# An attention and mixing kernel on one core: fixing the order in which TensorE issues, in long runs

## The chip, the cores and the metric

The kernel runs on one core of a Trainium2 chip. The metric is the device time of one execution in microseconds (us), of which the median of several runs is given. A profile of one execution shows what each engine did: TensorE (PE in the profile, and PEld for its weight loads), VectorE (DVE), ScalarE (ACT), GpSimd (POOL) and SyncE (SP), which issues the transfers.

## The reference

Eight batches of eight heads with 576 positions of 64 numbers go through causal attention with a window of 128 positions and a bias that falls with distance. The heads, side by side, are an x of 576 by 512 for each batch, and this x is mixed:

```
rel    = pos[:, None] - pos[None, :]
mask   = (rel >= 0) & (rel < 128)
scores = where(mask, q @ k.T / 8 - slope[h] * abs(rel), -1e9)
x      = softmax(scores) @ v                      # heads side by side: 576 x 512
theta  = x @ w_theta
y      = w_tok_r @ (x * cos(theta)) + w_tok_i @ (x * sin(theta))
u      = x + y
out    = u + max(u @ w_ch, 0)
```

## The kernel before, in words

The work of a batch has four stages, and the stages of neighbouring batches overlap.

**Attention**, in pairs of heads, four pairs to a batch (`attend`). For one pair: the scores (`Pair.scores`, L345 for the 64 last positions and L359 for the rest, 15 pieces of work in three calls that `SCORES` names), each with three products of rounded parts; the bias and the row minimum on DVE (`weigh`, L374, which reads the PSUM tile `s_ps`); the exponential on ACT (L377); the transposes of the weights (`flip`, L382, 16 for a pair in four banks), which ACT copies to half precision (L389) and DVE to the rest of it (L390); and for each of the two heads 27 products with v (`values`, L418) into the one PSUM tile `acc`, which DVE reads to divide by the sum (`finish`, L424 to L427) before the next head may write it. The scores of a pair are computed one pair ahead.

**The turn** (`turn`), once the four pairs of a batch are done: for each of five pieces i = 1, 2, 3, 4, 0 of the positions, four transposes of x (`columns`, L449), twelve products with w_theta (`products`, L469; eight for piece 0), and cosine and sine (`angle`, L480 to L501): ACT and DVE fold the angle into a turn (L483, L484, L486), ACT takes two sines (L490, L491), DVE multiplies them with x (L494), and each result is split into z_hi on ACT (L440) and z_lo on POOL (L441). Piece 0 is split apart from the others: L480, L481, L483, L484, L486, L490, L491, L498, L499, then z_hi on ACT (L500) and z_lo on DVE (L501). Pieces 1 to 4 give the chunks 0 to 7 of z, piece 0 gives chunk 8.

**Mixing** (`mix`): eight groups of 27 products (L530), three for each of the nine chunks in the order 0, 4, 1, 5, 2, 6, 3, 7, 8. Chunk 8 is the last of each group. When a group is done DVE adds it to x (L535), and ACT and POOL split the sum (L537, L538).

**Channels** (`channels`): eight groups of twelve products (L551), each closed by DVE (L554) and written out (L556).

While the pairs of batch b+1 are in `attend`, the mixing of batch b runs beside them, and the channels of batch b beside the turn of batch b+1. The table of ACT's functions is loaded twice for a batch: for the sines and, behind the last sine (`behind`), for the exponentials.

A scheduler orders each engine's instructions from the order of the program, priorities and its own estimate of times. Before, the priorities MIX, CHAN and ROTATE shift mixing, channels and turn against the attention, and `step(other, 6)` hands out pieces of mixing at three places of a pair. So TensorE's order is the scheduler's. PSUM has three banks for `mm` (theta, mixing, channels, the transposes of x, the first scores, the two small products of `spread`), two for `t_ps`, one `s_ps` of two banks, one `acc`.

The scales of v need the largest value of four heads (`measure`, L230), which reads the tile `vb` as soon as it is loaded; `vb` has two buffers, and a load waits until the heads in the older one are split (L311). ql (L292) is DVE's part in splitting q for the pair after the next.

## Time and profile before

| | |
|---|---|
| median of 3 runs | 764.3 us (763.7 to 765.51) |
| the profiled execution | 759.36 us, its span 757.5 us |
| PE, DVE, ACT, POOL busy | 706.1, 555.2, 478.1, 190.1 us |
| mean granted TensorE clock | 0.968 of full speed |
| read from HBM, written | 39.39 MB, 9.44 MB |

The profile gives for each group of instructions a line of the kernel, the engine, the tiles out<-in, the mean duration of one in ns and the idle time before it with the one that ended it. In the timeline a row has its start in us from the span's start, its length, and in brackets the idle time before it. A matmul's length contains the way through the array, so matmuls that follow each other overlap, and their pace is read from their starts.

### The profile page before, as it was taken

Reading aid. Unit: us, or ns where it says so; the run is one execution under the profiler, and the core shown is the slowest. Engines: PE = TensorE matmul, PEld = TensorE weight load, DVE = VectorE, ACT = ScalarE, POOL = GpSimd, SP = SyncE. Lnnn points to the kernel's source line nnn. Section 1 sums busy time; section 2 is a strip of 40 time slices with the busy share of each in tenths; the row PEclk is TensorE's granted clock in tenths of the full one; section 3 lists DMA queues with packets and bytes.
Section 4 is the critical chain, followed back from the end, with each engine's and each line's share of the span. In section 5 each row is a group of like instructions: output and inputs, shape, how many; then the busy total and the mean of one; then the engine's idle time right before and its main releaser. Section 6 shows DMA issues by size and latency. Waiting matters only on the chain.

```text
span 757.5 us, 16151 instructions
## 1 busy us (share of the span) xinstructions
PE 706.1 (93%) x6221; PEld 578.9 (76%) x6221; DVE 555.2 (73%) x1536; ACT 478.1 (63%) x948; POOL 190.1 (25%) x232
## 2 busy tenths in 40 slices
PE   4788987999999999899999999999999999999998
PEld 2466865788778887688878887788877887788887
DVE  6998768777779758786679757886679857864722
ACT  4896667755786566773787556873777556944610
POOL 2102214220431224121323214121323215111420
PEclk9768789999999999999999999999999999999999
DMA  9555201221022201221013201221013201000001
GB/s 311 170 158 168 64 14 33 67 84 40 32 85 61 73 29 55 67 84 41 23 49 99 76 25 56 75 75 49 24 48 99 68 32 46 19 2 32 32 1 63
DMA packets 32621, 49.87 MB, mean 66 GB/s; under 512 B 5664, under 2 KB 22048, under 8 KB 32544
## 3 DMA queue, kind: packets, MB, share of 16 engines
q1 hardware_dynamic: 32544, 48.84, 21.0%
q8 instruction: 49, 0.80, 0.5%
q14 instruction: 28, 0.23, 0.1%
HBM read 39.39 MB, written 9.44 MB: 64 GB/s over the span
## 4 chain that ended last, share of the span: by engine, by line
PE 48%; DVE 24%; ACT 16%; DMA 8%; issue 3%; POOL 0%; ACTq 0%; SPq 0%; DVEq 0%; POOLq 0%
PE mm L530 16%; PE mm L551 7%; PE mm L469 6%; PE acc L418 6%; PE s_ps L359 5%; PE t_ps L382 5%; DMA vb<-in_vx_dram 5%; DVE f L484 4%; ACT s_sb L377 4%; DVE g L486 3%; DVE g L494 2%; ACT g L490 2%; ACT f L483 2%; DVE s_sb L374 2%; DVE ql L292 2%
## 5 line engine op out<-in xcount | busy, mean ns | idle before, releaser
L530 PE MATMUL mm<-wtk_hi,z_hi 128*128 128x288 f16 x576 | 161.1, 287 | 4.6 <-DVE f L481 3.6
L530 PE MATMUL mm<-wtk_lo,z_hi 128*128 128x288 f16 x576 | 160.5, 286 | 0.0
L530 PE MATMUL mm<-wtk_hi,z_lo 128*128 128x288 f16 x576 | 158.3, 286 | 0.4 <-POOL z_lo L441 0.4
L530 PEld LDWEIGHTS <-z_hi 128*128 128x128 f16 x1152 | 108.2, 98 | 33.9 <-issue 5.0
L377 ACT ACTIVATE s_sb<-s_sb,fixed 128x256 f32<-128x256 f32 (+1 forms) x256 | 102.6, 470 | 15.1 <-DVE fixed L374 15.0
L538 POOL TENSOR_TENSOR u_lo<-xtf,u_hi 128x288 fp32r<-128x288 f32 x64 | 51.8, 816 | 192.5 <-ACT u_hi L537 171.9
L382 PE MATMUL t_ps<-fixed,s_sb 128*128 128x128 f32 x448 | 78.5, 286 | 9.8 <-ACT s_sb L377 3.0
L374 DVE CUSTOM_DVE_ANT_0 s_sb<-s_ps,bands 128x256 f32<-128x256 f32 (+1 forms) x256 | 85.3, 384 | 2.2 <-PE s_ps L359 2.2
L390 DVE SCALAR_TENSOR_TENSOR pt<-t_ps,pt 128x512 f16<-128x512 f32 x112 | 76.3, 685 | 11.6 <-ACT pt L389 11.6
L389 ACT ACTIVATE pt<-t_ps 128x512 f16<-128x512 f32 x112 | 65.3, 587 | 30.1 <-PE t_ps L382 29.5
L295 POOL TENSOR_TENSOR kl<-kr,kh 128x576 fp32r<-128x576 f32 x32 | 50.4, 1574 | 93.8 <-ACT kh L294 91.3
L441 POOL TENSOR_TENSOR z_lo<-g,z_hi 128x512 f16<-128x512 f32 x32 | 37.3, 1165 | 132.5 <-ACT z_hi L440 132.5
L530 PEld LDWEIGHTS <-z_lo 128*128 128x128 f16 x576 | 56.7, 99 | 14.4 <-POOL z_lo L441 0.9
L382 PEld LDWEIGHTS t_ps<-fixed,s_sb 128*128 128x128 f32 x448 | 52.7, 146 | 19.1 <-ACT s_sb L377 7.8
L418 PE MATMUL acc<-vh,pt 128*128 128x65 f16 x1008 | 65.2, 195 | 0.0
L418 PEld LDWEIGHTS <-pt 128*128 128x128 f16 x1512 | 59.4, 98 | 7.3
L537 ACT CAST u_hi<-xtf 128x288 fp32r<-128x288 f32 x64 | 27.3, 427 | 55.5 <-DVE xtf L535 55.3
L418 PE MATMUL acc<-vl,pt 128*128 128x64 f16 x504 | 56.0, 194 | 0.0
L490 ACT ACTIVATE g<-g,fixed 128x512 f32<-128x512 f32 (+1 forms) x40 | 29.0, 724 | 42.0 <-DVE g L486 41.5
L551 PE MATMUL mm<-u_hi,wch_hi 128*128 128x288 f32 x256 | 53.9, 322 | 1.0 <-DVE xtf L554 0.9
L469 PE MATMUL mm<-wth_hi,x_hi 128*128 128x512 f32 x160 | 46.7, 414 | 7.4 <-DVE f L484 7.4
L359 PE MATMUL s_ps<-kh,qh 64*128 64x256 f32 (+1 forms) x256 | 49.3, 342 | 3.5 <-DVE fixed L374 2.9
(139 smaller groups left out, 1561.1 us busy)
## 6 DMA issues: line engine op xcount, KB each, us to landing
vb<-in_vx_dram SPq DMA_DIRECT2D x16, 650.0 KB, 4.2
kr<-in_kt_dram SPq DMA_DIRECT2D x32, 288.0 KB, 2.9
out_dram<-xtf SPq DMA_DIRECT2D x64, 144.0 KB, 1.8
qr<-in_qt_dram SPq DMA_DIRECT2D x32, 144.0 KB, 2.8
qr<-in_qt_dram SPq DMA_DIRECT2D x32, 128.0 KB, 2.8
xtf<-in_wtok_dram SPq DMA_DIRECT2D x4, 576.0 KB, 3.9
u_hi<-in_wtok_dram SPq DMA_DIRECT2D x3, 576.0 KB, 3.8
u_lo<-in_wtok_dram SPq DMA_DIRECT2D x2, 576.0 KB, 6.1
```

The source lines that it names most:

```text
L295: nc.gpsimd.tensor_tensor(out=kl, in0=kr, in1=kh.bitcast(F32), op=ALU.subtract)
L359: nc.tensor.matmul(ps[:, e, off:off + kn], qm[rows, q0:q0 + qn], km[rows, k0:k0 + kn], start=(j == 0), stop=(j == last))
L374: nc.vector.tensor_tensor_reduce(out=sb, in0=ps, in1=bias, scale=2.0 ** -(2 * self.p % H + 1), scalar=3.0e38, op0=ALU.add, op1=ALU.min, ac ...
L377: self.exp = nc.scalar.activation(sb, sb, AF.Exp, bias=least, scale=-1.0)
L382: nc.tensor.transpose(t_ps[:, 128 * n:128 * n + 128], self.sc[i, e][:, 128 * j:128 * j + 128], ident)
L389: nc.scalar.activation(pt[:, 0], t_ps, AF.Copy, scale=2.0 ** PEXP)
L390: nc.vector.scalar_tensor_tensor(out=pt[:, 1], in0=t_ps, scalar=2.0 ** PEXP, in1=pt[:, 0], op0=ALU.mult, op1=ALU.subtract)
L418: nc.tensor.matmul(av[:, i, :r.shape[-1]], l, r, start=(n == 0), stop=(n == len(prods) - 1))
L469: nc.tensor.matmul(t_ps, a[:, c * 128:c * 128 + 128], w[:, c, :], start=(k == 0 and c == 0), stop=(k == len(prods) - 1 and c == 3))
L530: nc.tensor.matmul(y_ps[:, :HALF], z[:, c, m * 128:m * 128 + 128], w[:, c, cs], start=(k == 0), stop=(k == 26))
L538: nc.gpsimd.tensor_tensor(out=u_lo[:, m, cs], in0=xtf[:, m, cs], in1=u_hi[:, m, cs].bitcast(F32), op=ALU.subtract)
L551: nc.tensor.matmul(o_ps[:, :HALF], w[:, c, e * 128:e * 128 + 128], u[:, c, cs], start=(k == 0), stop=(k == 11))
```

## The change

From the first mixing on, every matmul and transpose that `mm` and `flipped` issue is held to the order of the program (`tc.keep_in_program_order`); the start of the kernel, up to and with the first turn, is left to the scheduler. The priorities and the helpers `urgent`, `ahead`, `ahead0` and `rotated` go. The program names TensorE's work in longer runs: for a pair 8 transposes (banks 0 and 2), the first 15 matmul steps of the scores, 27 products of mixing, the other 8 transposes (banks 1 and 3), 9 of mixing, the remaining scores, 9 of mixing, 27 products with v, 9 of mixing, 27 products with v; in the third and fourth pair a group of 12 channel products stands between the two heads. In the first pair, groups 0 and 1 of mixing are begun with chunks 0, 4, 1, 5, 2, 6 (18 products each) and closed later with chunks 3, 7, 8. `spread` is cut in two, with the transposes of the peaks ahead and the product later; `measure` stands earlier in the program. The transposes of x in the turn go to `t_ps` in place of `mm`. After the last attention, five mixing groups come first, then channels and mixing in turn. The matmuls themselves, their number and shapes stay.

```
+    pinned = []
+    def mm(*args, **kw):
+        ins = nc.tensor.matmul(*args, **kw)
+        if pinned:
+            tc.keep_in_program_order(ins)
...
-            x_ps = ps_m.tile([128, 512], F32, name="mm")
+            x_ps = ps_t.tile([128, 512], F32, name="t_ps")
...
+        def run(between):
+            order = (1, 2, 3, 4, 0)
+            between()
+            ahead = columns(order[0])
+            for j, i in enumerate(order):
+                between()
+                cur = ahead
+                if j + 1 < len(order):
+                    ahead = columns(order[j + 1])
+                theta(i, cur)
...
+        yield from part(0, range(6))
+        yield from part(1, range(6))
+        yield from part(0, range(6, 9))
+        yield from part(1, range(6, 9))
+        for g in range(2, 8):
+            yield from part(g, range(9))
...
             pair.flip(0)
-            pair.flip(1)
             pair.flip(2)
+            if g == 0:
+                step(mixing, 6)
             scores(SCORES[0])
             scores(SCORES[1])
-            step(other, 6)
+            if scaled:
+                measure(p // 2 + 1)
+            step(mixing, 6 if g == 0 else 9)
+            pair.flip(1)
+            pair.flip(3)
+            step(mixing, 3)
+            scores(SCORES[2])
+            if scaled:
+                spread_first(p // 2 + 1)
+            step(mixing, 3)
             one.values()
             one.finish(x_sb)
...
+            step(mixing, 3)
+            if g >= 2:
+                step(chans)
             two.values()
             two.finish(x_sb)
...
-    rotated(turn(x_sb, st[0]), iter(()))
+    turn(x_sb, st[0])(lambda: None)
+    pinned.append(True)
...
+            turn(x_sb, st[b + 1])(lambda: step(chans))
+            for _ in chans:
+                pass
+        else:
+            step(mixing, 45)
+            for _ in range(3):
+                step(chans)
+                step(mixing, 9)
```

Three places show what the change does to the engines' orders. The first is TensorE at the end of a turn, before: the last theta products (wth), channels (wch), the first scores of a coming pair (kh, ql, kl) and the first mixing (wtk).

```order
L469 MATMUL mm<-wth_hi,x_hi 128x512 x4
L469 MATMUL mm<-wth_lo,x_hi 128x512 x4
L551 MATMUL mm<-u_lo,wch_hi 128x288
L551 MATMUL mm<-u_hi,wch_hi 128x288 x4
L551 MATMUL mm<-u_hi,wch_lo 128x288 x4
L551 MATMUL mm<-u_lo,wch_hi 128x288 x4
L345 MATMUL mm<-kh,qh 128x192
L345 MATMUL mm<-kh,ql 128x192
L345 MATMUL mm<-kl,qh 128x192
L530 LDWEIGHTS z_hi
L530 MATMUL mm<-wtk_hi,z_hi 128x288
```

The same place after, where `mm` and `flipped` have lines 69 and 74, and t_ps takes the transposed weights of a pair.

```order
L69 MATMUL mm<-u_hi,wch_lo 128x288 x4
L69 MATMUL mm<-u_lo,wch_hi 128x288 x4
L69 MATMUL mm<-wth_hi,x_hi 128x512 x4
L69 MATMUL mm<-wth_lo,x_hi 128x512 x4
L74 MATMUL t_ps<-fixed,last_106 128x128 x2
L74 MATMUL t_ps<-fixed,s_sb_5666 128x128 x3
L74 MATMUL t_ps<-fixed,s_sb_5667 128x128 x3
L69 LDWEIGHTS z_hi
L69 MATMUL mm<-wtk_hi,z_hi 128x288
```

The channel group and the scores no longer stand between the last theta product and the mixing; eight transposes do. After these rows TensorE has 18 products of group 0 (chunks 0, 4, 1, 5, 2, 6), 15 score steps, 18 products of group 1, eight transposes and the nine products of group 0 with the chunks 3, 7 and 8, in this order.

The second place is ACT behind the same turn, before: the sines of piece 0 (L490, L491), the table of the exponentials, nine exponentials (L377) and z_hi of chunk 8 (L500).

```order
L490 ACTIVATE g<-g,fixed 64x512
L491 ACTIVATE f<-f 64x512
L377 ACT_TABLE_LOAD
L377 ACTIVATE last_106<-last_106,fixed 128x192
L377 ACTIVATE s_sb_4926<-s_sb_4926,fixed 128x128
L377 ACTIVATE s_sb_4927<-s_sb_4927,fixed 128x128
L377 ACTIVATE s_sb_4926<-s_sb_4926,fixed 128x256
L377 ACTIVATE s_sb_4927<-s_sb_4927,fixed 128x256
L377 ACTIVATE s_sb_5014<-s_sb_5014,fixed 128x256
L377 ACTIVATE s_sb_5015<-s_sb_5015,fixed 128x256
L377 ACTIVATE s_sb_5014<-s_sb_5014,fixed 128x256
L377 ACTIVATE s_sb_5015<-s_sb_5015,fixed 128x256
```

After, the sines are lines 507 and 508, the exponentials line 394, and z_hi of chunk 8 line 517.

```order
L497 COPY g<-mm 64x512
L406 ACTIVATE pt<-t_ps 128x512 x2
L457 CAST z_hi<-g 128x512
L457 CAST z_hi<-f 128x512
L500 ACTIVATE g<-f 64x512
L507 ACTIVATE g<-g,fixed 64x512
L508 ACTIVATE f<-f 64x512
L394 ACT_TABLE_LOAD
L394 ACTIVATE last_104<-last_104,fixed 128x192
L394 ACTIVATE s_sb_6192<-s_sb_6192,fixed 128x128
L394 ACTIVATE s_sb_6193<-s_sb_6193,fixed 128x128
L394 ACTIVATE s_sb_6192<-s_sb_6192,fixed 128x256
```

One more exponential follows, and then L517. The two copies of transposed weights (L406) now stand ahead of the splits of piece 4 (L457) and of piece 0's angle, and five exponentials in place of nine ahead of z_hi of chunk 8.

The third place is DVE in the second pair of a batch, at the first head's `finish`. Before:

```order
L390 SCALAR_TENSOR_TENSOR pt<-t_ps,pt 128x512
L232 TENSOR_SCALAR peak_107<-peak_107 128x4
L424 TENSOR_SCALAR fixed<-acc,fixed 128x5
L426 RECIPROCAL fixed<-fixed 128x5
L311 SCALAR_TENSOR_TENSOR vl<-vb,fixed,vh 128x320
L427 TENSOR_TENSOR x_sb<-acc,fixed 128x5x64
```

After, with the last of the four minima of the third scores (L391, a custom instruction), the closing of mixing group 3 (L562) and ql (L309) ahead of it.

```order
L391 ISA s_sb_6510,fixed<-s_ps,bands 128x256
L391 ISA fixed 128x1
L562 SCALAR_TENSOR_TENSOR xtf<-mm,fixed,xtf 128x288
L309 SCALAR_TENSOR_TENSOR ql<-qr,fixed,qh 128x640
L441 TENSOR_SCALAR fixed<-acc,fixed 128x5
L443 RECIPROCAL fixed<-fixed 128x5
L444 TENSOR_TENSOR x_sb<-acc,fixed 128x5x64
```

The reading of `acc` by L444, which the second head's products wait for, has moved behind the closing of a mixing group and behind ql, while on TensorE the second head now follows the first after nine products of mixing.

More of the change, by code (lines that the diff above doesn't have):

```diff
@@ L241, in spread, with spread_to @@
         nc.vector.tensor_scalar(out=diag, in0=ident[:, :n], scalar1=whole, scalar2=None, op0=ALU.mult)
+        return diag
+    def spread_to(diag, n, part):
         w_ps = ps_m.tile([128, 512], F32, name="mm")
-        nc.tensor.matmul(w_ps[:, :n], ones.broadcast_to([128, 128]), diag, start=True, stop=True)
+        mm(w_ps[:, :n], ones.broadcast_to([128, 128]), diag, start=True, stop=True)
         scale = rings["scale" + part].take()
@@ L344, in scores @@
                 for j, (qm, km) in enumerate(self.terms):
[L345 removed]
+                    mm(ps[:, :kn], qm[:, 512:], km[:, k0:k0 + kn], start=(j == 0), stop=(j == last))
                 whole = lasts[self.p % len(lasts)]
@@ L468, in products @@
                 for c in range(4):
-                    nc.tensor.matmul(t_ps, a[:, c * 128:c * 128 + 128], w[:, c, :], start=(k == 0 and c == 0),
+                    mm(t_ps, a[:, c * 128:c * 128 + 128], w[:, c, :], start=(k == 0 and c == 0),
                                      stop=(k == len(prods) - 1 and c == 3))
@@ L502, in angle, with theta @@
                                                op0=ALU.mult, op1=ALU.subtract)
-        order = (1, 2, 3, 4, 0)
-        ahead = columns(order[0])
-        yield
-        for j, i in enumerate(order):
-            cur = ahead
-            if j + 1 < len(order):
-                ahead = columns(order[j + 1])
-            yield
+        def theta(i, parts):
             t_ps = ps_m.tile([128, 512], F32, name="mm")
-            products(t_ps, *cur)
+            products(t_ps, *parts)
             angle(i, t_ps)
-            yield
+        def run(between):
[8 more added lines that the diff above has]
+                theta(i, cur)
+        return run
     def mix(st):
@@ L522, in mix, with part @@
         st.update(u_hi=u_hi, u_lo=u_lo)
-        for hf in range(2):
-            for m in range(4):
-                cs = slice(hf * HALF, hf * HALF + HALF)
-                y_ps = ps_m.tile([128, 512], F32, name="mm")
-                k = 0
-                for c in ORDER:
-                    for z, w in ((z_hi, wtk_hi), (z_hi, wtk_lo), (z_lo, wtk_hi)):
-                        nc.tensor.matmul(y_ps[:, :HALF], z[:, c, m * 128:m * 128 + 128], w[:, c, cs],
-                                         start=(k == 0), stop=(k == 26))
-                        k += 1
-                    if k < 27:
-                        yield
+        banks = {}
+        def part(g, ks):
+            hf, m = divmod(g, 4)
+            cs = slice(hf * HALF, hf * HALF + HALF)
+            if g not in banks:
+                banks[g] = ps_m.tile([128, 512], F32, name="mm")
+            y_ps = banks[g]
+            for k in ks:
+                c = ORDER[k]
+                for n, (z, w) in enumerate(((z_hi, wtk_hi), (z_hi, wtk_lo), (z_lo, wtk_hi))):
+                    mm(y_ps[:, :HALF], z[:, c, m * 128:m * 128 + 128], w[:, c, cs],
+                       start=(k == 0 and n == 0), stop=(k == 8 and n == 2))
+                if k < 8:
+                    yield
+            if ks[-1] == 8:
                 nc.vector.scalar_tensor_tensor(out=xtf[:, m, cs], in0=y_ps[:, :HALF], scalar=st["back"],
@@ L578, in step, with attend @@
             next(stream, None)
-    def urgent(stream, offset):
-        while True:
-            with tc.high_priority(offset) if offset else nullcontext():
-                try:
-                    next(stream)
-                except StopIteration:
-                    return
-            yield
-    def attend(b, x_sb, other, first, behind):
+    def attend(b, x_sb, mixing, chans, first, behind):
         for g in range(H // 2):
@@ L599, in attend @@
                 first.append(new)
+            scaled = p % 2 == 0 and p + 2 < pairs
             def scores(tiles):
@@ L614, in attend @@
                 new.heads[0].ready()
-            pair.flip(3)
-            scores(SCORES[2])
-            if p % 2 == 0 and p + 2 < pairs:
-                measure(p // 2 + 1)
-            step(other, 6)
+            step(mixing, 3)
+            if g >= 2:
+                step(chans)
             two.values()
             two.finish(x_sb)
-            if p % 2 == 0 and p + 2 < pairs:
+            if scaled:
                 spread_scales(p // 2 + 1)
@@ L626, in attend @@
                 new.heads[1].ready()
-            step(other, 6)
     def start(x_sb, load):
@@ L679, in start @@
             pass
-    def ahead(prods, chans):
-        for k, _ in enumerate(prods):
-            if k in AHEAD:
-                next(chans)
-            yield
-    def ahead0(prods, chans):
-        yield from prods
-        for _ in range(AHEAD0):
-            next(chans)
-            yield
-    def rotated(rotate, chans):
-        step(rotate, 2)
-        for _ in range(NT):
-            step(chans)
-            step(rotate, 2)
-        for _ in chans:
-            pass
     first = []
```

50 lines of the change are left out of this document (28 added, 22 removed).

## The prediction

> **What bounds the kernel now.** I read the page first, then the busy time of one inner batch, then who waited for whom on TensorE in it, then the timeline of three engines at the end of a turn.
>
> ```profile
> PE 706.1 (93%) x6221; PEld 578.9 (76%) x6221; DVE 555.2 (73%) x1536; ACT 478.1 (63%) x948; POOL 190.1 (25%) x232
> PEclk9768789999999999999999999999999999999999
> ```
>
> TensorE is busy for 93% of the span and its clock is full from about 190 us on. The next view is an inner batch, from one first mixing product to the next: length, busy time and number of matmuls, clock, DMA share, GB/s.
>
> ```profile
> 467.49:553.33 85.84, 83.33 (x782) 1.00 0.19 58
> ```
>
> In 85.84 us TensorE is idle for 2.5. Its waits in this stretch (total us, times, longest) say where:
>
> ```profile
> PE mm L530 <- DVE f L481: 1.2, 2, 0.6
> PE mm L469 <- DVE f L484: 1.0, 2, 0.5
> ```
>
> Both are waits for a PSUM bank that DVE has not yet read. So a batch is bound by TensorE: by its matmuls, by what it pays when their kind changes, and by hardly anything else. The scheduler has ordered it so that the other engines are nearly always ahead. What a fixed order can win is the price of the changes and these 2.5 us; what it can lose is that a matmul which isn't ready now holds up all behind it.
>
> **Prices of TensorE's work.** Starts that follow each other in a run give the pace: theta products, channel products, then the first mixing.
>
> ```profile
> 462.85 1.08 PE L469 MATMUL mm<-wth_hi,x_hi 128*128 128x512 f32 x4
> 463.77 1.08 PE L469 MATMUL mm<-wth_lo,x_hi 128*128 128x512 f32 x4
> ...
> 464.82 0.70 PE L551 MATMUL mm<-u_hi,wch_hi 128*128 128x288 f32 x4
> ...
> 466.42 0.25 PE L345 MATMUL mm<-kh,qh 128*128 128x192 f32 x1
> ...
> 467.49 0.28 PE L530 MATMUL mm<-wtk_hi,z_hi 128*128 128x288 f16 x1 [0.60 <-DVE f L481]
> 467.62 0.28 PE L530 MATMUL mm<-wtk_lo,z_hi 128*128 128x288 f16 x1
> ```
>
> Four theta products take 0.92, so 0.23 each; twelve channel products 1.60; a mixing product 0.12. A run of 27 products with v, four transposes, a run of twelve score steps, scores between mixing, and channels between products with v:
>
> ```profile
> 434.90 0.20 PE L418 MATMUL acc<-vh,pt 128*128 128x65 f16 x1
> ...
> 435.15 0.20 PE L418 MATMUL acc<-vh,pt 128*128 128x65 f16 x1
> ...
> 437.30 0.39 PE L359 MATMUL s_ps<-kh,qh 64*128 64x256 f32 x2
> ...
> 438.21 0.30 PE L530 MATMUL mm<-wtk_hi,z_hi 128*128 128x288 f16 x1
> ...
> 439.81 0.60 PE L449 MATMUL mm<-fixed,x_sb 128*128 128x128 f32 x4
> ...
> 472.22 0.33 PE L359 MATMUL s_ps<-kh,ql 64*128 64x128 f32 x2
> 472.48 0.30 PE L530 MATMUL mm<-wtk_lo,z_hi 128*128 128x288 f16 x1
> ...
> 476.33 0.19 PE L418 MATMUL acc<-vh,pt 128*128 128x65 f16 x1
> ...
> 477.15 0.41 PE L382 MATMUL t_ps<-fixed,s_sb 128*128 128x128 f32 x2
> ```
>
> 27 products with v take 0.82, or 0.03 each; a transpose about 0.11; twelve score steps 0.91 with the way out. A lone pair of score steps costs 0.26 until the next mixing, against 0.15 for a sixth of the run, and the way in is of the same size: about 0.2 for a change in and out. One product with v and one with channels take 0.25 where a run of each has 0.03 and 0.13: 0.09 for the change.
>
> **The change, part by part.** *Fewer changes of kind.* By the two orders a batch has 16 runs of scores before and 8 after, and 10 changes from products with v to channels before and 2 after: 8 x 0.2 + 8 x 0.09 = 2.3 us saved. Added up from the prices above, TensorE's own work of a batch after is 76.8 us (below, leg by leg); before it is 83.3. The 4.2 us that lie between, beyond the 2.3, are short pauses which the lengths of the matmuls cover; I take it that long runs lose them too, and keep them for the upper end of the range.
>
> *The transposes of x in the banks of t_ps* leave the three mm banks to theta, channels and mixing. The waits of L469 go. The transfer costs nothing, since no weights of a pair are transposed during the turn; without that cover the pair's first transposes would wait for ACT's copies of x. The turn is then TensorE's own work: 6 x 1.60 + 56 x 0.23 + 20 x 0.11 = **24.7 us** from the last product with v to the last theta product.
>
> *Chunk 8.* Here the new order waits. These are ACT's rows at the end of a turn (start, length): piece 0's copy, its first step, its sine, the table, the exponentials, z_hi of chunk 8.
>
> ```profile
> 465.58 0.58 ACT L480 COPY g<-mm 64x512 f32<-64x512 f32 x1
> ...
> 468.71 0.61 ACT L483 ACTIVATE g<-f 64x512 f32<-64x512 f32 x1
> 472.01 0.72 ACT L490 ACTIVATE g<-g,fixed 64x512 f32<-64x512 f32 x1 [2.69 <-DVE g L486]
> ...
> 473.27 1.28 ACT L377 ACT_TABLE_LOAD   x1
> 474.57 0.45 ACT L377 ACTIVATE last<-last,fixed 128x192 f32<-128x192 f32 x1
> 474.93 3.07 ACT L377 ACTIVATE s_sb<-s_sb,fixed 128x128 f32<-128x128 f32 x8
> 477.91 0.71 ACT L500 ACTIVATE z_hi<-g,fixed 128x512 f16<-128x512 f32 x1
> ```
>
> And DVE's long step of piece 0, and its z_lo of chunk 8, which ends the chain:
>
> ```profile
> 469.64 1.88 DVE L484 SCALAR_TENSOR_TENSOR f<-g,f 64x512 f32<-64x512 f32 x1
> ...
> 478.65 0.75 DVE L501 SCALAR_TENSOR_TENSOR z_lo<-g,fixed,z_hi 128x512 f16<-128x512 f32 x1 [1.74 <-ACT z_hi L500]
> ```
>
> The last theta product ends at 463.77 + 1.08 = 464.85, z_lo at 479.40: 14.5 us later. Before, nothing waits for it, since other work stands ahead of the products with chunk 8. After, four exponentials fewer precede z_hi (3.07 / 8 x 4 = 1.5 less); but ACT and DVE come to piece 0 about 1 us later in relation to TensorE, which no longer waits in the turn, and the copies of two banks replace two splits of k and q there. I take 14.0 us, between 13 and 15, and 0.3 for the last products: 14.3. TensorE's own work in front is 16 transposes (1.8), 45 mixing products (5.5) and 15 score steps (1.2): 8.5. So it waits **5.8 us in every batch** (4.5 to 6.8), and 9 products, 12 score steps and both heads are queued behind.
>
> *The two heads of a pair.* They share `acc`, and only 9 mixing products (1.1 us), or 12 channel products in the third and fourth pair, now stand between them. DVE's prices:
>
> ```profile
> L390 DVE SCALAR_TENSOR_TENSOR pt<-t_ps,pt 128x512 f16<-128x512 f32 x112 | 76.3, 685 | 11.6 <-ACT pt L389 11.6
> L374 DVE CUSTOM_DVE_ANT_0 s_sb<-s_ps,bands 128x256 f32<-128x256 f32 x192 | 71.4, 418 | 0.5 <-PE s_ps L359 0.5
> L535 DVE SCALAR_TENSOR_TENSOR xtf<-mm,fixed,xtf 128x288 f32<-128x288 f32 x64 | 32.6, 511 | 16.3 <-PE mm L530 15.8
> L292 DVE SCALAR_TENSOR_TENSOR ql<-qr,fixed,qh 128x640 fp32r<-128x640 f32 x32 | 31.9, 996 | 6.5 <-ACT qh L291 6.5
> L427 DVE TENSOR_TENSOR x_sb<-acc,fixed 128x320 f32<-128x320 f32 x64 | 31.3, 489 | 1.4
> ```
>
> DVE's instructions overlap by 0.08, so I count each 0.08 less. In the first pair, from z_lo of chunk 8 to the release of acc: two rests of transposes 1.2, mixing group 0 closed 0.4, four minima 1.4, group 1 closed 0.4, ql 0.9, small ones 0.4, `finish` 0.95 (0.49 and two small ones): 5.6. TensorE needs 4.1 (0.9 + 1.1 + 0.8 + 1.1, small 0.2): it waits 1.5. The second and fourth pairs also read a new `vb`:
>
> ```profile
> 482.29 0.55 DVE L311 SCALAR_TENSOR_TENSOR vl<-vb,fixed,vh 128x320 f16<-128x320 f32 x1
> ...
> 487.07 1.49 DVE L230 TENSOR_REDUCE peak<-vb 128x4 f32<-128x1280 f32 x1 [0.76 <-DMA vb<-in_vx_dram]
> ```
>
> The load starts when the old buffer's last split (L311) ends and L230 begins 4.2 us later. From the end of the pair before: `finish` and split 1.9, load 4.2, L230 1.4, closing a group 0.6, two rests with ACT's copy between them 1.6, minima 1.4, closing 0.4, ql 0.9, `finish` 0.95: 13.3. TensorE's own work there is 11.4 in the second pair, 11.9 in the fourth: waits of 1.9 and 1.4. The third pair, 13.8, waits for nothing.
>
> *Moved at no cost*: the peaks' transposes and the small product of `spread` stand between longer runs, with several us until their result is used; on SP the load of `vb` stands ahead of those of k and q and behind an output whose channel group is closed before the load's own buffer is free. If an output came later than the last split, the 13.3 above would grow by as much.
>
> *Sum of an inner batch*: turn 24.7, chunk 8 14.3, then 5.6 + 0.8, 13.3 + 0.8, 13.8, 13.3 + 0.8 (0.8 is each second head): **87.4 us, against 85.8**.
>
> *The clock.* Two windows of the early kernel show what a pause does (length, busy, count, clock):
>
> ```profile
> 126.10:129.50 3.40, 1.29 (x14) 1.00 0.00 0
> 129.50:132.90 3.40, 3.24 (x28) 0.50 0.00 0
> ```
>
> A stretch of 3.4 us with TensorE busy for 1.29 is followed by one at half clock. A wait of 5.5 us in one piece holds such a stretch wherever it falls. Half clock for some 3 us after it delays TensorE by 1.5, of which the waits for DVE in the first pair swallow part: 1.0 us a batch, between 0 and 2.5. [...]
>
> *All batches*, against the profiled execution of 759.4: five inner batches x (1.6 + 1.0) = 13.0; the mixing of the first batch, which has waits of its own to lose, -2 (-5 to +2); that of the seventh, where the last two `vb` waits are missing but the wait for chunk 8 isn't, 0 (-2 to +3); the last one, without attention, has only 42 mixing products (5.1 us) ahead of chunk 8 and a chain without exponentials of some 11, so +4 (0 to +6). Together +15: 774.4. The median of the runs lies 0.65% above the profiled execution, and so I put the forecast: **779 us**.
>
> **The rivals.** (a) *Faster*: only chunk 8 is waited for, because DVE gets through a pair sooner than I add up; the pairs' 4.8 us go. An inner batch is then 82.6 + 1.0, which is 2.2 below before: 5 x -2.2 - 7 + 4 = -14, 745 by the profile, **750**. For it: DVE is only 73% busy. Against: its orders have the closing of a group and ql ahead of `finish`. It decides where the waits of a batch come to 2.5 us less than summed. (b) *No change*: the pairs wait half as long; an inner batch is 85.0 + 1.0, the first batch's -4 and the last one's +4 cancel, the whole +1: **765**. (c) *Far slower*: the short pauses remain in part (2 us) and the half clock lasts two stretches (1 more): 5 x 5.6 + 3 + 2 = +33 at most, 798; the case is put midway between this and my sum: **788**. (d) The order isn't held: the two orders show that it is.
>
> **How the numbers follow.** A measurement of this kernel tells a difference of 0.2%, 1.5 us, from none. My sum 0.54, (a) 0.21, (b) 0.14, (c) 0.10, (d) 0.01. (b) splits into same 0.07 and 0.035 to each side; (d) is same. Faster 0.24, same 0.08, slower 0.68. The range reaches from (a) at 750 to 793, midway in (c)'s upper half; of my own sum alone it is 767 to 791, from the chain of chunk 8 (1 us), the pairs (1 us) and the clock (1 us) in each batch.
>
> **What would show it.** Right: in each batch one TensorE wait of about 5 us for z_hi of chunk 8 (L517) and one of 0.5 for z_lo (L518); waits of 1 to 2 us of products with v for L444 in the first, second and fourth pair; a clock below 1.00 once in each batch, and a mean below 0.968; no theta product waiting for DVE. Wrong: a wait for chunk 8 under 3 us, or no waits for L444: then the other engines' orders gave more room than I read in them.

## The result, and the profile after

The changed kernel takes 782.42 us in the median of 4 runs (780.71 to 784.19), the one before 764.21 (763.7 to 765.51) beside it: a ratio of 1.0236 with a 95% interval of 1.0208 to 1.0264. The profiled execution took 783.17 us, with a span of 781.4 and a mean clock of 0.934 where it was 0.968.

The page of the changed kernel, busy time of TensorE and its clock in 40 slices:

```profile
PE 696.9 (89%) x6221; PEld 583.6 (75%) x6221; DVE 560.0 (72%) x1536; ACT 479.2 (61%) x948; POOL 189.5 (24%) x232
PEclk9786597999989999999989998999989999999999
```

TensorE is busy for 9 us less than before and yet the span is 24 longer; the clock now falls below full again and again. Who TensorE waits for in the whole execution (total us, times, longest):

```profile
PE mm L69 <- ACT z_hi L517: 32.2, 8, 4.3
PE acc L69 <- DVE x_sb L444: 15.2, 18, 1.8
PE mm L69 <- DVE z_lo L518: 1.3, 4, 0.4
```

L69 is now the line of every product, so the tiles say which it is: mixing waits for z_hi of chunk 8, once in each of the eight batches, and products with v wait for `finish` of the other head. From the first mixing on, no theta product waits for DVE. Stretches of the changed kernel: a turn, an inner batch from last theta product to last theta product, and the seventh batch (length, busy, matmuls, clock, DMA share, GB/s):

```profile
447.53:472.43 24.90, 24.90 (x156) 1.00 0.13 44
472.40:560.20 87.80, 81.28 (x785) 0.96 0.19 57
648.20:732.40 84.20, 78.80 (x752) 0.96 0.07 22
```

The turn is TensorE's own work from end to end. An inner batch takes 87.8 us where it took 85.8. The place where it stands still, on TensorE:

```profile
471.36 1.07 PE L69 MATMUL mm<-wth_lo,x_hi 128*128 128x512 f32 x4
...
480.35 0.29 PE L69 MATMUL mm<-wtk_hi,z_lo 128*128 128x288 f16 x1
484.95 0.42 PE L69 MATMUL mm<-wtk_hi,z_hi 128*128 128x288 f16 x1 [4.32 <-ACT z_hi L517]
...
492.72 0.20 PE L69 MATMUL acc<-vh,pt 128*128 128x65 f16 x1 [0.44 <-DVE x_sb L444]
```

The last theta product ends at 472.43; 8.2 us of work follow, then a pause of 4.3. What ACT does meanwhile (last sine, table, exponentials, z_hi of chunk 8, the copies of the first pair's transposes):

```profile
480.52 0.61 ACT L508 ACTIVATE f<-f 64x512 f32<-64x512 f32 x1
481.16 1.28 ACT L394 ACT_TABLE_LOAD   x1
482.45 0.45 ACT L394 ACTIVATE last<-last,fixed 128x192 f32<-128x192 f32 x1
482.81 1.47 ACT L394 ACTIVATE s_sb<-s_sb,fixed 128x128 f32<-128x128 f32 x4
484.19 0.70 ACT L517 ACTIVATE z_hi<-g,fixed 128x512 f16<-128x512 f32 x1
484.81 1.05 ACT L406 ACTIVATE pt<-t_ps 128x512 f16<-128x512 f32 x2
```

And DVE behind it, from z_lo to the release of acc:

```profile
484.93 0.75 DVE L518 SCALAR_TENSOR_TENSOR z_lo<-g,fixed,z_hi 128x512 f16<-128x512 f32 x1 [2.64 <-ACT z_hi L517]
485.60 1.28 DVE L407 SCALAR_TENSOR_TENSOR pt<-t_ps,pt 128x512 f16<-128x512 f32 x2
...
490.34 0.52 DVE L562 SCALAR_TENSOR_TENSOR xtf<-mm,fixed,xtf 128x288 f32<-128x288 f32 x1 [0.89 <-PE mm L69]
490.78 0.88 DVE L309 SCALAR_TENSOR_TENSOR ql<-qr,fixed,qh 128x640 fp32r<-128x640 f32 x1
...
492.18 0.49 DVE L444 TENSOR_TENSOR x_sb<-acc,fixed 128x320 f32<-128x320 f32 x1
```

acc of the first head comes free at 492.67, 20.2 us after the last theta product. That number is the one to keep for what follows. The clock around the pause, in stretches of 3.41 us:

```profile
480.06:483.47 3.41, 0.57 (x5) 1.00 0.00 0
483.47:486.88 3.41, 1.80 (x9) 0.50 0.00 0
486.88:490.29 3.41, 3.41 (x24) 0.50 0.00 0
490.29:493.70 3.41, 2.97 (x66) 1.00 0.50 133
```

A stretch with 0.57 us of work is followed by two at half clock, 6.8 us. So it is in four of the five inner batches; in one there is a single such stretch. The half clock reaches back into DVE's rows: between z_lo and the release of acc, DVE waits 0.89 us for a mixing group (L562) that TensorE works off at half clock, and 0.47 for scores.

Where the 23.8 us between the two profiled executions came from, by the ends of the last theta products of each turn (worked out from the timelines):

| part | before | after | difference | predicted |
|---|---|---|---|---|
| up to the end of the first turn | 115.5 | 115.0 | -0.5 | - |
| first batch of mixing | 89.8 | 93.2 | +3.5 | -2 |
| five inner batches | 431.2 | 440.0 | +8.8 | +13 |
| seventh | 75.9 | 84.2 | +8.2 | 0 |
| last, without attention | 41.9 | 45.8 | +3.9 | +4 |

### The profile page after: what moved, and what is told of

It is laid out like the page before. It is cut to its first block, busy times and chain, and to the rows that moved or that the text cites. A ratio compares the mean times of both kernels' runs of the same rounds, so it can differ in the third digit from the quotient of the medians.

```text
span 781.4 us, 16125 instructions
## 1 busy us (share of the span) xinstructions
PE 696.9 (89%) x6221; PEld 583.6 (75%) x6221; DVE 560.0 (72%) x1536; ACT 479.2 (61%) x948; POOL 189.5 (24%) x232
## 4 chain that ended last, share of the span: by engine, by line
PE 53%; DVE 20%; ACT 18%; DMA 4%; issue 4%; POOL 0%; SPq 0%; DVEq 0%; ACTq 0%; POOLq 0%
PE mm L69 32%; PE acc L69 7%; PE t_ps L74 7%; PE s_ps L69 6%; DVE g L503 4%; ACT g L507 3%; DVE f L501 3%; DVE s_sb L391 2%; ACT f L508 2%; DVE ql L309 2%; ACT f L500 2%; ACT z_hi L457 2%; ACT s_sb L394 1%; DVE x_sb L444 1%; ACT L507 1%
## 5 line engine op out<-in xcount | busy, mean ns | idle before, releaser
L69 PE MATMUL mm<-wtk_hi,z_hi 128*128 128x288 f16 x576 | 170.5, 296 | 33.9 <-ACT z_hi L517 32.2
L69 PE MATMUL mm<-wtk_hi,z_lo 128*128 128x288 f16 x576 | 169.8, 295 | 4.2 <-POOL z_lo L458 2.4
L69 PE MATMUL mm<-wtk_lo,z_hi 128*128 128x288 f16 x576 | 169.8, 295 | 0.0
L69 PEld LDWEIGHTS <-z_hi 128*128 128x128 f16 x1152 | 110.8, 101 | 68.4 <-ACT z_hi L517 34.5
L391 DVE CUSTOM_DVE_ANT_0 s_sb<-s_ps,bands 128x256 f32<-128x256 f32 (+1 forms) x256 | 84.4, 384 | 10.0 <-PE s_ps L69 9.9
L407 DVE SCALAR_TENSOR_TENSOR pt<-t_ps,pt 128x512 f16<-128x512 f32 x112 | 74.7, 683 | 21.7 <-ACT pt L406 21.7
L458 POOL TENSOR_TENSOR z_lo<-g,z_hi 128x512 f16<-128x512 f32 x32 | 37.5, 1173 | 181.8 <-ACT z_hi L457 181.8
L406 ACT ACTIVATE pt<-t_ps 128x512 f16<-128x512 f32 x112 | 62.1, 591 | 23.5 <-PE t_ps L74 22.0
L69 PEld LDWEIGHTS <-z_lo 128*128 128x128 f16 x576 | 57.9, 101 | 24.4 <-DVE z_lo L518 5.3
L312 POOL TENSOR_TENSOR kl<-kr,kh 128x576 fp32r<-128x576 f32 x32 | 46.1, 1439 | 123.6 <-ACT kh L311 123.6
L69 PEld LDWEIGHTS <-pt 128*128 128x128 f16 x1512 | 54.5, 100 | 22.0 <-issue 11.3
L69 PE MATMUL acc<-vh,pt 128*128 128x65 f16 x1008 | 58.0, 198 | 14.3 <-DVE x_sb L444 14.3
L74 PE MATMUL t_ps<-fixed,s_sb 128*128 128x128 f32 x448 | 64.0, 281 | 2.1 <-ACT pt L402 1.8
L326 ACT ACTIVATE vh<-vb,fixed 128x320 f16<-128x320 f32 x56 | 31.1, 557 | 51.0 <-PE acc L69 51.0
L69 PE MATMUL acc<-vl,pt 128*128 128x64 f16 x504 | 54.2, 196 | 0.0
L562 DVE SCALAR_TENSOR_TENSOR xtf<-mm,fixed,xtf 128x288 f32<-128x288 f32 x64 | 32.8, 513 | 29.3 <-PE mm L69 29.3
L69 PE MATMUL mm<-wth_hi,x_hi 128*128 128x512 f32 x160 | 47.8, 422 | 2.2 <-DVE x_hi L473 1.8
```

What stands on the lines that cost most here:

```text
L69: ins = nc.tensor.matmul(*args, **kw)
L74: ins = nc.tensor.transpose(*args)
L312: nc.gpsimd.tensor_tensor(out=kl, in0=kr, in1=kh.bitcast(F32), op=ALU.subtract)
L391: nc.vector.tensor_tensor_reduce(out=sb, in0=ps, in1=bias, scale=2.0 ** -(2 * self.p % H + 1), scalar=3.0e38, op0=ALU.add, op1=ALU.min, ac ...
L406: nc.scalar.activation(pt[:, 0], t_ps, AF.Copy, scale=2.0 ** PEXP)
L407: nc.vector.scalar_tensor_tensor(out=pt[:, 1], in0=t_ps, scalar=2.0 ** PEXP, in1=pt[:, 0], op0=ALU.mult, op1=ALU.subtract)
```

## The experiments

The first theory was the prediction's: the held order makes TensorE wait for chunk 8, lowers its clock behind that, and makes second heads wait for acc; the loss is the sum of these. The rival: DVE and ACT are late whatever TensorE does, and its waits are only where that shows.

Each kernel is a change of the changed one. The ratio is to the kernel before, run beside it; the changed kernel's own is 1.0236. The stage times are told together behind the first eight.

**z_hi ahead of the exponentials.**

```
-                nc.scalar.activation(z_hi[:, 8, :], g, AF.Copy, scale=zs[:, 8:9])
+                st["sin"] = nc.scalar.activation(z_hi[:, 8, :], g, AF.Copy, scale=zs[:, 8:9])
```

> Theory (the fixed order waits for chunk 8, whose z_hi stands behind the table load and five exponentials on ACT): with z_hi of chunk 8 ahead of them its source on DVE is ready about 1.9 us sooner than ACT gets to it now, so the wait for L517 falls from 4.3 to 2.1-2.4 us in a batch; 2.0 x 8 = 16 less, 766 us. If a pause of 2.3 us no longer lowers the clock, another 1.6 x 8 = 13 less, 754. Rival (the time only moves: the exponentials and the copies of the first pair, now later on ACT, are waited for instead): 776 or more, with a new wait on ACT of 2 us in each first pair.

786.02 us, 1.0275 (1.0234 to 1.0317): no gain. The wait for z_hi falls from 32.2 to 17.7 in all, and that for L444 rises from 15.2 to 31.3. The wait moves, as the rival said (though to L444 on DVE and not to ACT), and ACT's rows of this run show how:

```profile
391.53 0.72 ACT L517 ACTIVATE z_hi<-g,fixed 128x512 f16<-128x512 f32 x1 [1.18 <-DVE g L516]
392.27 1.28 ACT L394 ACT_TABLE_LOAD   x1
...
395.31 1.05 ACT L406 ACTIVATE pt<-t_ps 128x512 f16<-128x512 f32 x2
```

Its last theta product ended at 381.64. z_hi is done 10.6 us after that, not 12.5; but the table and the exponentials now stand ahead of the copies of the first pair's transposes, which end 14.7 us after it where they ended 13.4 after it. acc comes free 19.7 us after the last theta product, only 0.5 sooner.

**Chunk 8 not waited for.**

```
-                    mm(y_ps[:, :HALF], z[:, c, m * 128:m * 128 + 128], w[:, c, cs],
+                    mm(y_ps[:, :HALF], z[:, min(c, 7), m * 128:m * 128 + 128], w[:, c, cs],
```

This kernel leaves out what chunk 8 adds to the mixing; its products read chunk 7 instead.

> Leaves out the contribution of chunk 8 to the mixing: its products read chunk 7 in its place, with the same number and shapes of matmuls, so nothing on TensorE waits for the end of piece 0. Theory: the whole price of chunk 8 goes, 4.3 + 0.3 of waiting and about 1.7 of half clock in each of 8 batches (50), of which the first pair's wait for acc takes back 1 a batch: 782 - 42 = 740 us, mean clock back above 0.96. Rival 1 (DVE and ACT set the pace and the wait only shows where PE stands idle for them): 770 or more, with the waits for L444 and for pt longer by 3 us or more a batch. Rival 2 (the wait counts, the clock after it doesn't): 757.

779.63 us, 1.0191 (1.0137 to 1.0246): 3 us less where 42 were forecast, and the two intervals overlap. This is the experiment that broke the first theory. TensorE's waits in it:

```profile
PE acc L69 <- DVE x_sb L444: 28.7, 21, 3.7
...
PE acc L69 <- ACT pt L406: 10.3, 6, 1.7
PE acc L69 <- DVE pt L407: 6.9, 7, 1.1
```

46 us, where the changed kernel has 49 for z_hi, L444 and z_lo: nearly the same waiting, only later. DVE's rows say why; the last theta product of this batch ended at 386.60:

```profile
399.09 0.75 DVE L518 SCALAR_TENSOR_TENSOR z_lo<-g,fixed,z_hi 128x512 f16<-128x512 f32 x1 [2.65 <-ACT z_hi L517]
...
405.12 0.49 DVE L444 TENSOR_TENSOR x_sb<-acc,fixed 128x320 f32<-128x320 f32 x1
```

TensorE no longer needs chunk 8, but DVE still works through its row in the same order: z_lo, the rests of the transposes, the closings, ql, then `finish`. acc comes free 19.0 us after the last theta product. So it is the first rival in the main: of a wait of 4.3 us, 1.2 are won.

A part of the rest goes to the clock. The pause now stands ahead of the second head, so half clock falls on the second pair, where TensorE works without a break. Here is its block from the second head to the third, in the batch above and in a later one, where the half clock ends before it (length, busy, matmuls, clock, DMA share, GB/s):

```profile
405.70:419.00 13.30, 13.30 (x117) 0.78 0.24 72
494.80:505.40 10.60, 10.60 (x118) 1.00 0.30 90
```

The first of these batches takes 89.1 us, the later one 86.6; the mean of the changed kernel is 88.0.

**Dummy work in the pause.**

```
+            step(mixing, 2 if g == 0 else 3)
+            if g == 0:
+                fill(18)
+                step(mixing, 1)
```

(`fill` writes these products into `s_ps`, the bank of the scores.)

> Adds 18 dummy products (about 0.21 us each at full clock, 3.9 us) on TensorE in the pause ahead of the products with chunk 8 in each first pair (seven batches), so that the pause itself stays and only the clock after it changes. Theory: the clock stays at 1.00; the scores, the mixing and the products with v behind the pause take 1.5 to 2 us less, of which the wait for acc in the first pair takes back about 1: 0.5 to 1.0 x 7 = 4 to 7 less, 776 to 779 us. Rival (half clock costs nothing, since DVE and ACT set the pace behind the pause): 782 or more. Rival (the clock is the larger part of the loss, over 2 us a batch): 768 or less.

788.43 us, 1.0321 (1.0267 to 1.0375): no gain, though the mean clock rises to 0.945. In the inner batches the clock behind the pause now stays full until the second head, and acc comes free after 19.7 us in place of 19.8 to 20.3: the half clock there had cost it 0.6 us at most. But the second head still waits for acc (25.1 us for L444 in all, 15.2 before), and half clock comes later, mostly in the second pair. Its block from the second head to the third, in an inner batch where half clock doesn't fall on it and in one where it does:

```profile
226.20:236.90 10.70, 10.70 (x119) 1.00 0.31 94
493.80:506.10 12.30, 12.23 (x117) 0.86 0.27 84
```

One stretch of half clock costs 1.6 us there. So the dummy work moves the half clock and doesn't remove it; what a full clock throughout would be worth is not shown.

**More mixing between the heads.**

```
-            step(mixing, 6 if g == 0 else 9)
+            step(mixing, 6 if g == 0 else 3)
...
-            step(mixing, 3)
+            step(mixing, 9)
```

(the second is the one between the heads)

> Only moves six steps of mixing (18 products, 2.2 us) in the second to fourth pair, and adds six in the first, from ahead of the first head to between the two heads. Theory (the second head waits for the acc of the first): the waits for L444, 15.2 us in all, fall to under 4; 782 - 11 = 771 us, since chunk 8 and its clock stay. Rival (DVE is behind as a whole, so the wait goes to another place: products with v then wait for pt of L407, or the first head for the transposes): 778 or more, with new waits of 1 us for pt in each pair.

788.67 us, 1.03 (1.0247 to 1.0352). The waits for L444 don't fall (18.3 in place of 15.2). Those of 1 us for pt in each pair, which the rival named, don't show either (1.8 in all for L407).

After these four the theory was put anew: what counts is when DVE and ACT are done behind the turn, not where TensorE stands idle for them.

**Piece 0 first**, so that the last chunks have no table load ahead of them.

```
-            order = (1, 2, 3, 4, 0)
+            order = (0, 1, 2, 3, 4)
...
-                c = ORDER[k]
+                c = (8, 0, 4, 1, 5, 2, 6, 3, 7)[k]
```

> Piece 0 goes first in the turn and chunk 8 first in each mixing group, so the last chunks are those of piece 4, which has no table load or exponentials ahead of its z_hi. New theory (after the turn DVE and ACT are behind with their own work, and the second head's acc comes free 20 us after the last theta product whether TensorE waits for chunk 8 or not; 15.7 us of DVE's work lie there): the wait for chunk 8 goes, and acc comes free 2 to 4 us sooner since DVE no longer stands idle for z_hi; 2 to 4 x 7 = 14 to 28 less than 782, 754 to 768 us. First theory (the waits of TensorE add up): 739. Rival (DVE's work after the turn is simply put in another order): 778 or more, with longer waits for pt and L444.

762.57 us, 0.9976 (0.9942 to 1.001): 20 us less than the changed kernel, as the new theory said, with the order held all the same. The last theta product of a batch, and the first release of acc after it:

```profile
461.99 1.07 PE L69 MATMUL mm<-wth_hi,x_lo 128*128 128x512 f32 x4
```

```profile
479.87 0.48 DVE L444 TENSOR_TENSOR x_sb<-acc,fixed 128x320 f32<-128x320 f32 x1
```

480.35 - 463.06 = 17.3 us, and a batch of 85.5. It is the first that moves this number by more than 1.2 us, and the first with a gain clear of the noise. Its inner batches have one stretch of half clock or none, so a part of the gain may be the clock's.

**The same program, the order not held.**

```
-    pinned.append(True)
```

> The changed program, but TensorE's order is never held: the scheduler orders it by its own estimate, with no priorities. If the loss lies in holding the order (work of the first pair and mixing can't be moved to where DVE and ACT are late): 755 to 770 us, no wait for chunk 8 and more changes of kind. If it lies in the order in which the program names its work, and the scheduler alone would follow it: 775 to 790.

743.98 us, 0.9758 (0.9699 to 0.9818): faster than expected, and faster than the kernel before. The changed program is the better one; holding its order costs 4.8% of the time before (38 us). Its inner batch and its clock:

```profile
374.90:458.30 83.40, 81.41 (x784) 1.00 0.20 60
```

```profile
PEclk9786579999999999999999999999999999999999
```

TensorE waits 2.0 us in 83.4, at full clock. The changed kernel waits 6.5 in 87.8 and loses some 2.5 to half clock. Against that, TensorE's own work is 81.4 here and 78.8 there; I take the difference to be changes of kind, which the free order has more of. DVE's row has another order behind the last theta product, which ended at 374.87:

```profile
387.46 0.49 DVE L444 TENSOR_TENSOR x_sb<-acc,fixed 128x320 f32<-128x320 f32 x1
...
388.87 0.75 DVE L518 SCALAR_TENSOR_TENSOR z_lo<-g,fixed,z_hi 128x512 f16<-128x512 f32 x1
```

acc is released 13.1 us after it, and ahead of z_lo of chunk 8. On TensorE the scheduler puts the first head's products with v (382.74) ahead of all products with chunk 8, whose z_hi is done at 388.84, and 23 score steps and four transposes of the coming pairs into the turn. On ACT two copies of transposes (377.52 and 379.09) stand ahead of the table load (382.30).

**Two channel groups behind the turn.**

```
+                step(late, 2)
...
+            places = iter((1, 1, 0, 1, 0, 1) if b + 2 < B else (1,) * 6)
+            turn(x_sb, st[b + 1])(lambda: step(chans, next(places)))
+            late = chans
```

> Two of the six groups of channel products in each turn (six turns) are issued behind its last theta product, ahead of the first mixing. New theory (TensorE sets the time of the turn, 24.7 us, with DVE and ACT busy for 16 of them; behind it DVE and ACT set it): the turn is 3.2 us shorter, and the time from the last theta product to acc grows by at most 1.5, since the two groups stand in TensorE's wait: 1.7 to 3.2 x 6 = 10 to 19 less, 763 to 772 us. Rival (the angles set the pace: ACT and DVE finish piece 0 when they did before, only counted from an earlier theta product): 780 or more, with the wait for chunk 8 at 1.1 us and that for L444 3 us longer.

772.62 us, 1.012 (1.0069 to 1.0172): some 10 us less, half a us above the range of the new theory. The theta products take 17.6 us where they took 20.9, and acc comes free after 20.0 us as ever. Part of the gain is lost again: the clock is 0.86 over the block from the second head to the third, and the third starts 1.6 us later than in the changed kernel.

**Three mixing groups begun.**

```
+        for g in range(3):
+            yield from part(g, range(8))
+        for g in range(3):
+            yield from part(g, (8,))
+        for g in range(3, 8):
```

(and the steps of mixing in `attend` are handed out to match)

> Three mixing groups are begun with all chunks but 8 in the first pair (72 products ahead of chunk 8 in place of 42) and closed there, and a fourth stands between its heads; the third and fourth pair have half the mixing. New theory (a batch is a chain of stages, some bound by TensorE, some by DVE): the wait for chunk 8 falls to 0.7 or less, the clock stays at 1.00, the first pair ends 0 to 1.5 us later, the second is unchanged at 13.9, the third, bound by TensorE at 14.0, loses 2 to 3.3, the fourth 0.5: 1.5 to 3.5 x 6 = 9 to 21 less, 761 to 773 us. Rival (DVE sets the time of each pair, the third too, by its 10.5 us of work and the waits in it): 778 or more.

782.25 us, 1.0249 (1.0195 to 1.0303): no gain, and so the new theory was wrong here. The third pair does get 2.3 us shorter, but the first head now stands behind 72 products of mixing, which themselves wait for z of the earlier chunks (L458, 15.7 us in all); acc comes free after 22.6 us or more. (The execution profiled here took 793.87 us, far above the median, so its stage times are rough.)

The stage times of all these, in us from the end of a batch's last theta product (worked out from the timelines; ranges are over inner batches, and the last column has where half clock begins in them):

| kernel | acc first free | second head | third head | last head | next last theta product | half clock from |
|---|---|---|---|---|---|---|
| changed | 19.8-20.3 | 19.9-20.4 | 30.5-31.1 | 61.7-63.0 | 87.5-88.7 | 11-13 |
| z_hi first | 19.7 | 19.8 | 30.4-32.2 | 62-66 | 87.2-92.1 | 11-13, 20-37 |
| no chunk 8 | 19.0 | 19.1 | 29.7-32.9 | 60.9-63.8 | 86.6-89.6 | 14-20 |
| dummy work | 19.7 | 19.7 | 30.4-33.6 | 62.7-64.8 | 88.4-90.5 | 20-21, in one 35 |
| mixing between heads | 20.0 | 21.6 | 30.1 | 63.0 | 88.7 | 10 |
| piece 0 first | 17.5 | 17.6 | 28.2 | 60 | 84.9-86.1 | 11-12, in one none |
| channels behind | 20.0 | 20.1 | 32.3-33.3 | 63.1-64.0 | 85.5-86.5 | 19-21 |
| three groups begun | 22.6-24.0 | 24-25.5 | 32.4-33.9 | 63-64.5 | 88.8-91.8 | 7, in two also 65 |
| not held | 13.1 | 13.2 | 19.0 | 56.8 | 83.4 | none |

In every held kernel at least 8.4 us pass from the second head to the third: one block of transposes, scores and mixing that nothing may interrupt. It takes 10.6 at full clock (8.4 where 18 of its products of mixing stand elsewhere) and up to 13.9 with half clock on it. In the free order it is 5.8. So the first theories both have a part: what DVE and ACT still have to do keeps acc back, and the half clock that the waits bring costs most where it falls on this block. The next question was which half of the held order costs.

**Held in the second to fourth pair only.**

```
+            pinned[:] = [True] if g else []
```

(and cleared behind the last pair)

> TensorE's order is held in the second to fourth pair only, as in the changed kernel; the turn and the first pair are the scheduler's, which puts twelve score steps of the coming pairs and four transposes into the turn and eleven score steps behind the first head. Theory (the loss lies behind the turn: DVE has 16 us of work in the 25 of the turn and then too much, because no work of the pairs may pass the turn): nearly all of the gain of the free order stays, 744 to 752 us, no wait for chunk 8 over 1 us in an inner batch. Rival (the loss lies in the pairs, where the free order also moves work): 770 or more.

774.3 us, 1.0098 (1.0056 to 1.014). The theory was wrong: acc does come free after 13.1 us, as in the free order, but less than a third of the gain stays. The third head starts 26.5 to 29.2 us after the last theta product, not 19.0. Between the heads of the first pair TensorE has nothing that it may issue, since the scores and transposes behind them are held. In one batch:

```profile
392.75:396.15 3.40, 1.26 (x9) 0.99 0.00 0
396.15:405.85 9.70, 8.61 (x63) 0.50 0.34 102
399.51:402.92 3.41, 3.04 (x15) 0.50 0.14 17
```

With a pause of 2.1 us and one of 0.9 the clock is 0.50 for 10 us, and here that falls on the held block of the second pair, which TensorE itself bounds: 8.6 us of work at half speed, an estimated 4 us lost in this batch. (The last row is the middle third of the half clock.)

**Held in the turn and the first pair only.**

```
+            pinned[:] = [] if g else [True]
```

(and set behind the last pair)

> The reverse: held in the turn and the first pair, the second to fourth pair are the scheduler's. Theory: the wait for chunk 8 (4.3) and the second head's wait in the first pair stay, the free pairs win 0 to 1.5 us a batch at their waits for L444: 772 to 784 us. Rival (the loss lies in the pairs): 755 or less. If both halves cost, this one and the one that holds the pairs add up: their losses against 744 together make 38.

783.13 us, 1.0268 (1.0201 to 1.0334): as slow as with all of it held. acc comes free after 20.2 us, the last head starts at 63.1. Against the free order the two halves cost 3.4% and 5.1%, together 8.5%, where holding both costs 4.8%. So they don't add: either half is enough to lose most of it.

**Twelve score steps ahead, order held.**

```
+                if len(calls) == 6 and b + 2 < B:
+                    nxt = Pair((b + 2) * H // 2 + DEPTH), []
+                    nxt[0].scores(SCORES[1], None, nxt[1])
+                step(chans)
```

(and `attend` leaves these steps out and takes the exponentials alone)

> All of the order is held, but one run is written in another place: the twelve score steps of the second and third tile of the coming pair stand in the turn, ahead of its last channel group, in place of behind it in the first pair (six turns); DVE takes their four minima there, and ACT's exponentials stay behind the last sine. Theory (what counts is how much of DVE's work lies behind the turn, not that the order is held): 1.4 us of minima leave the stage that DVE bounds, and TensorE's own work there falls by 1.0: 1.4 to 3 x 6 = 8 to 18 less than 782, 764 to 774. Rival (holding the order costs by itself, or the minima hold up the angles in the turn by as much): 779 or more.

789.11 us, 1.0327 (1.0278 to 1.0377): the rival. On DVE the four minima (the first and last are shown) stand between two steps of piece 4, and on ACT the copies of the first pair's transposes now come ahead of z_hi (L523 here):

```profile
386.40 0.28 DVE L391 CUSTOM_DVE_ANT_0 s_sb<-s_ps,bands 128x128 f32<-128x128 f32 x1
...
387.17 0.42 DVE L391 CUSTOM_DVE_ANT_0 s_sb<-s_ps,bands 128x256 f32<-128x256 f32 x1
387.51 0.42 DVE L509 TENSOR_SCALAR g<-f 128x512 int32<-128x512 int32 x1
```

```profile
398.68 1.05 ACT L412 ACTIVATE pt<-t_ps 128x512 f16<-128x512 f32 x2
399.63 0.71 ACT L523 ACTIVATE z_hi<-g,fixed 128x512 f16<-128x512 f32 x1
```

The longest wait for z_hi grows from 4.3 to 5.6 us. So less of DVE's work behind the turn isn't enough by itself. These rows suggest that what stands ahead of the angles and ahead of `finish` on DVE and ACT counts, but the run doesn't tell the minima's part from the copies'.

**Not held, and piece 0 first.**

(the edits of both earlier kernels together)

> The changed program with a free order and piece 0 first in the turn, chunk 8 first in each group. The free order waits only 2 us in an inner batch of 83.45, 0.5 of it for chunk 8, so there is little left to win there: 0 to 0.5 x 6, and 2.9 + 3.9 in the first and last batch where chunk 8 is still waited for: 737 to 744 us. Rival (the scheduler's order gets worse, since the angles now end with a whole piece on ACT and DVE): 748 or more.

727.87 us, 0.9526 (0.9466 to 0.9585): the fastest, 4.7% below the kernel before, and better than expected. Its page:

```profile
PE 680.1 (94%) x6218; PEld 574.6 (79%) x6221; DVE 551.3 (76%) x1536; ACT 477.1 (66%) x948; POOL 186.7 (26%) x232
PEclk9787589999999999999999999999999999999999
```

Four of the five inner batches take 81.3 us, 2.1 less than in the free order alone, which waited only 2.0. TensorE's busy time falls by 1.6 in one of them; which changes of kind this order saves wasn't taken apart. The first release of acc comes 16.3 us after the last theta product, later than the 13.1 of the free order alone. So that number by itself doesn't rank kernels.

## Why the prediction was right, and where its working wasn't

The direction is right, and the waits on TensorE are the ones forecast; the forecast of 779 lies 3 us below the result. Several terms were off and cancelled, so that it came so near is luck.

*Fewer changes and TensorE's own work.* 76.8 us was put for a batch. Measured: 81.28 busy, of which some 2.5 are half clock (5.2 us between 484.95 and 490.29 at half speed), so 78.8. The long runs gave 4.5 us, not 6.5: about half of the "short pauses" stay.

*The turn.* 24.7 put, 24.9 measured, and no theta product of an inner batch waits for DVE. Right.

*Chunk 8.* The chain was put at 14.0 and measured 13.25 (485.68 - 472.43), the work in front at 8.5 and 8.2. The wait was put at 5.8, with 4.5 as its lower end, and is 4.3 plus 0.1 to 0.4 for z_lo. Mechanism right, size at the lower end.

*The two heads.* Put: 1.5, 1.9, 0 and 1.4. Measured in the batch shown: 0.4, 1.0, 0 and 0.6, so 2.1 where 4.8 were put. The first is small because the half clock made TensorE later, and DVE waited for it: from z_lo to the release of acc it took 7.0 us, not the 5.6 of the sum.

*The clock.* Put at one stretch of half clock and 1.0 us; it is two stretches, 6.8 us, in four of five inner batches, and the 2.5 us it takes were in part swallowed by the wait for acc, as the prediction said. In the batch shown 0.57 us of work in 3.41 didn't keep the clock up, and it fell in every one of the inner batches (to 0.50, for one stretch of 3.41 us in the second and for two in the others).

*The sum of an inner batch.* 87.4 + 1.0 = 88.4 was put, the mean is 88.0. By legs the stretch up to z_lo of chunk 8 was put 1 us too long and the rest of the first pair 1.5 too short, as half clock stands in it; the turn and the other pairs are within 0.3. So the method, which takes the longer of TensorE's work and the other engines' chain in each leg, holds, and a part of the agreement is cancellation. The five together cost 8.8 more than before and not the 13 that were put: 2.2 of the 4.2 between lie in the kernel before, one of whose inner batches takes 88.1 us and not 85.8.

*All batches.* This step failed. The seventh was put at 0 and costs 8.2, the first at -2 and costs 3.5. Two rows of the kernel before show what was overlooked: the stretch of its seventh batch, and the start of 27 products within its first turn.

```profile
636.50:712.40 75.90, 73.55 (x686) 1.00 0.08 25
```

```profile
93.73 0.19 PE L418 MATMUL acc<-vh,pt 128*128 128x65 f16 x1
93.76 0.19 PE L418 MATMUL acc<-vl,pt 128*128 128x64 f16 x1
```

Products with vl exist only from the fifth pair on. So the kernel before has done the first head of the next batch, with its transposes and scores, before the theta products of the turn begin, and it keeps this lead to the end: 686 matmuls in its seventh batch, 752 after the change. It paid for them at the start, where TensorE had time: 534 matmuls are done by the end of its first turn, after 115.5 us, and 467 in the changed kernel after 115.0. The held order begins each batch's attention behind the turn and has no lead. The scale from the profiled execution to the median (0.65%) failed too: 782.42 lies 0.1% below the profiled 783.17. The sum was 9 us too low and the scale added 5; that is how 779 came near, by luck.

What the experiments add to the prediction's reasons is a limit. It named the waits for chunk 8 and for acc, and both are there; but they are where the delay shows, not what it is worth to remove. Taking away the first moved most of it into the second, which my own sum could have told: 14.3 and then 5.6 us are DVE's time, whatever TensorE waits for in it. It also moved the half clock into a block that TensorE bounds. What is shown is that the loss comes with holding the order (743.98 without), that one change which lets acc come free 2.7 us sooner under a held order wins (762.57), and that holding either half is enough to lose most of it. How much of the loss is half clock and how much the engines' order was not separated. What stays open too is which of the moves across the turn carries the free order's gain: the one tried, twelve score steps, doesn't, and moving the first head ahead of chunk 8 by hand, or the copies of its transposes ahead of the table load, wasn't tried.

## What to carry to other kernels

Write the program in long runs, and time it with the order free before you hold it: here the program alone was worth 2.4% and holding it cost 4.8%. Before you price a wait, ask when the engine waited for is done with all that stands in its row up to the next release, for here a wait removed in front of another one on the same engine mostly moved. And when orders are compared, look at how far one batch's work reaches into the next, at the first and the last batch too.

## What of the hardware was unexpected

Half clock lasted beyond the pauses: with one of 4.3 us (480.64 to 484.95 in the changed kernel) came 6.8 us at a clock of 0.50 (483.47 to 490.29), 5.3 of them behind its end, and with two of 0.9 and 2.1 us close together came 10 (second to fourth pair held). In that last case a stretch of 3.41 us with 3.04 us of work at half clock was followed by another at half clock, while one that was filled throughout (486.88 to 490.29 in the changed kernel) was the last. But of two more in the changed kernel the one with 3.21 us of work (309.39 to 312.80) was the last, and the one with 3.24 (220.65 to 224.06) was followed by another, so how much work ends it isn't shown. What half clock cost was not the same everywhere: with the dummy work at most 0.6 us for the release of acc behind the pause, where DVE and ACT set the pace, and 1.6 us for one stretch in a block that TensorE bounds (12.30 us for 10.70).
